# A token-mixing block: z's broadcast behind a q tile, and the low parts of w1 behind `ol`

## The chip, the cores and the metric

The kernel runs on one core of a Trainium2 chip. The metric is the device time of one execution in microseconds. The engines are named as the profile names them: PE (TensorE's matmuls) and PEld (its weight loads), DVE (VectorE), ACT (ScalarE), POOL (GpSimd) and SP (SyncE, which only issues DMAs here).

## The reference

Two blocks follow each other on a sequence of 2048 tokens with 512 channels, in float32. Shown is the core of it; the first block is attention with 32 heads of 16 channels, the second an MLP over the tokens.

```python
h = x + A(layernorm(x)); h2 = h + B(layernorm(h))

# A: linear attention with a learned feature map
q, k, v = split_heads(x @ wqkv)
pq, pk = q @ w_phi, k @ w_phi                      # per head, 16 x 16
phi_q = concat(softmax(pq), softmax(-pq))          # 32 features per head
phi_k = concat(softmax(pk), softmax(-pk))
kv = phi_k^T v;  z = sum over tokens of phi_k
o = (phi_q kv) / (phi_q . z + 1e-6);  out = o @ wo

# B: MLP across the tokens
u = gelu(h^T w1 + b1);  y = u w2 + b2              # w1 2048 x 1792, w2 1792 x 2048
```

## The kernel before, in words

**Numbers in two parts.** Large matmuls run on pairs of float32r tiles: a high part, which ScalarE copies out of the float32 source, and a low part, source minus high part, which VectorE or GpSimd subtracts. `split` (line 54) issues both. `mm3` (line 59) makes one product of three matmuls: high by high, high by low, low by high. So every weight that is streamed from memory costs a ScalarE copy (`whi`, line 56) and a subtraction (`wlo`, line 57).

**Stages.** The 2048 tokens are 16 tiles of 128.
1. Preparation and a loop over k and v tiles (lines 216 to 414): k's projection, its logits (maximum and minimum of each head, two subtractions), exp, sums, normalization on GpSimd (`pk`, line 193) and the sum z over the tiles in `zacc`; v's projection, and kv on TensorE (`kvp`, line 205). Six q tiles are projected in this loop too.
2. A hand-over (lines 416 to 509). The last k and v tiles are finished, wo is split into `woh` (ScalarE, line 426) and `wol` (GpSimd, line 429), and z is broadcast to all partitions: two matmuls of ones with the halves of `zacc` (line 486) and two copies into `zB` (line 487). From here on `ez`, the product of a q tile's features with `zB` on GpSimd (line 440), can be made. q tiles 6, 7, 8 and 9 are projected in this stretch.
3. A software pipeline over the q tiles (the loop `for it in range(NT + 3)`, line 620), described below.
4. The rest of the first MLP matmul (lines 707 to 715), the second one with w2 streamed (from line 756), and the output.

**Who decides the order.** In stage 1 and stage 4 a planner orders each engine's instructions. From line 417 to line 653 the order on PE, DVE, ACT and POOL is that of the program text, `manual_schedule`; each engine takes its instructions strictly in that order. SP's DMAs are ordered by the planner.

**A q tile's way.** `q_mm` projects it into PSUM (tile `pu`, a pool of two buffers, so tile n+2 goes where tile n was). `q_logits` takes the maximum `mx` and the minimum `mn` (lines 151, 152) and subtracts on DVE (line 144); from tile 6 on, the negative half is copied by ACT out of PSUM (line 146) and subtracted later on POOL by `negate` (line 159), to which the list `MN` holds what is due. `q_exp` (line 169, ACT) follows. `q_sums` takes sums on DVE (line 214). `s_den` makes the weights `w` of a tile from `ez` (six DVE instructions, from `tz`, line 449, to `w`, line 455). `s_pq` multiplies the tile by them on POOL (`eq<-eq,w`, line 458).

**One iteration of the loop**, `it`, in order:
- `s_x(it)`: DMA of a tile of x. `s_rstd(it-3)` on POOL: `r` (line 578) and `ve` (line 579).
- `s_num(it-1)`: 32 small matmuls into the PSUM tile `tn` (line 544), and ACT copies its high part, `oh` (line 548).
- `s_wo(it-2)`: 12 matmuls with wo into the one PSUM buffer `po`.
- `s_tr(it)`: 8 transposes into the same `tn` (line 526), two ACT copies `pht` (line 528). They wait until `oh` and `ol` have been read out.
- `lead(it, 1)`: `s_pq(it+1)`, `s_ez(it+3)` and `negate` on POOL, the next `q_mm` on PE, `q_exp` on ACT.
- `run(...)` (line 638): it takes one instruction from each of its lists in turn. The first list is `ol` (DVE subtracts the low part out of `tn`, line 553), then the next tile's logits, then the sums; the second list is `s_den(it+2)`. Then `negate`.
- `s_hn(it-3)`: the normalized tile `hn` and its split `hs`, the low part on POOL (line 57).
- `s_h(it-2)`: DVE adds x to `po` (`h`, line 568, which frees `po`), a DMA stores it, and DVE takes its statistics (`st`, `ve`, lines 571 to 575).
- `fill(p)`: six matmuls of the first MLP product for a pair of hidden blocks; and `fill_load(p)` every second time: `stream` loads two 128x256 blocks of w1, ACT makes `whi`, DVE makes `wlo`, a 128x512 subtraction at line 57. The loads of one iteration's end serve fills that come two iterations later.

In iteration 1 a further q tile is projected between `s_num` and `s_tr` (line 631); it is tile 11.

Of the kernel before, what the change touches and what calls it, by code (L numbers as in the profile page):

```python
# [11 lines left out]
AF = mybir.ActivationFunctionType  # L12
# [7 lines left out]
NT = S // P  # L20
KD = D // P
# [12 lines left out]
def block_kernel(ctx: ExitStack, tc: tile.TileContext, x, xT, wT, phic, wo, w1, b1, w2, b2,  # L34
                 kvmask, ident_in, out):
    nc = tc.nc
# [17 lines left out]
    def split(hi, lo, src, lo_engine):  # L54

        nc.scalar.activation(hi, src, AF.Copy)  # L56
        return lo_engine.tensor_sub(lo, src, hi)  # L57

    def mm3(o, ah, al, bh, bl, first, last):

        nc.tensor.matmul(o, ah, bh, start=first, stop=False)  # L61
        nc.tensor.matmul(o, ah, bl, start=False, stop=False)  # L62
        nc.tensor.matmul(o, al, bh, start=False, stop=last)  # L63
# [24 lines left out]
    zacc = wp.tile([P, NG, P], F32, name="zacc")  # L88
# [5 lines left out]
    X, XH, EQ, PK, VS, SQ, PS, W = {}, {}, {}, {}, {}, {}, {}, {}  # L94

    def load_x(t):
        raw = kk.tile([P, KD, P], F32, name="xraw", bufs=3)
        nc.sync.dma_start(raw, xT[t])
        return raw
# [18 lines left out]
    def proj(t, wh, wl, pool, name, by_part=False):  # L118
        o = pool.tile([P, D], F32, name=name, tag=name)
        if by_part:  # L120
            for i, (a, w) in enumerate(((0, wh), (1, wh), (0, wl))):
                for kt in range(KD):
                    nc.tensor.matmul(o, X[t][:, a, kt, :], w[:, kt, :], start=i == 0 and kt == 0,
                                     stop=i == 2 and kt == KD - 1)
            return o
        for kt in range(KD):
            mm3(o, X[t][:, 0, kt, :], X[t][:, 1, kt, :], wh[:, kt, :], wl[:, kt, :],
                kt == 0, kt == KD - 1)
        return o
# [6 lines left out]
    def logit_ops(src, e, pool):  # L136

        v = src.rearrange("p (j h d) -> p j h d", h=2, d=DH)
        ev = signs(e)
        mx = wk.tile([P, NPR, 2], F32, name="mx")  # L140
        mn = wk.tile([P, NPR, 2], F32, name="mn")

        def shift():
            nc.vector.tensor_sub(ev[:, :, 0], v, mx.unsqueeze(3).to_broadcast([P, NPR, 2, DH]))
            if pool:
                nc.scalar.activation(ev[:, :, 1], v, AF.Copy)  # L146
                MN.append((ev, mn))
            else:
                nc.vector.tensor_sub(ev[:, :, 1], mn.unsqueeze(3).to_broadcast([P, NPR, 2, DH]), v)

        return [lambda: nc.vector.tensor_reduce(mx, v, axis=AX.X, op=ALU.max),
                lambda: nc.vector.tensor_reduce(mn, v, axis=AX.X, op=ALU.min),
                shift]

    def negate():

        if MN:
            ev, mn = MN.pop(0)
            nc.gpsimd.tensor_sub(ev[:, :, 1], mn.unsqueeze(3).to_broadcast([P, NPR, 2, DH]), ev[:, :, 1])

    def run(*lists):

        for i in range(max(map(len, lists))):
            for ops in lists:
                if i < len(ops):
                    ops[i]()
# [42 lines left out]
    def q_sum(t):  # L209

        assert t < SUMS or t - SUMS in W, "a tile's sums would go where others are still wanted"
        SQ[t] = sums[:, t % SUMS]
        e = signs(EQ[t])
        return [lambda c=c: nc.vector.reduce_sum(SQ[t][:, :, 1 - c], e[:, :, c], axis=AX.X) for c in range(2)]
# [144 lines left out]
    def q_mm():  # L359
        if q["mm"] < NT:  # L360
            PS[q["mm"]] = proj(q["mm"], wqh, wql, ps_q, "pu")
            q["mm"] += 1

    def q_logits(lag):
        n = q["logits"]
        if n < min(NT, q["mm"] - lag + NT * (q["mm"] == NT)):
            EQ[n] = big.tile([P, NG, P], F32, name="eq", tag="big")
            q["logits"] += 1
            return logit_ops(PS[n], EQ[n], n >= len(Q_AT))
        return []  # L370
# [7 lines left out]
    def q_sums(lag):  # L378
        n = q["sum"]
        if n < min(NT, q["exp"] - lag + NT * (q["exp"] == NT)):  # L380
            q["sum"] += 1
            return q_sum(n)
        return []

    def v_kv():

        nonlocal v
        v_proj(v)
        if v % 2 == 0:
            kv(v - 2)  # L390
            kv(v - 1)
        v += 1
# [4 lines left out]
    for t in range(3, NT - 1):  # L397
        if t + 2 < NT:
            raw = load_x(t + 2)
# [25 lines left out]
    def wo_hi(j):  # L425
        nc.scalar.activation(woh[:, j], WO[j], AF.Copy)

    def wo_lo(j):
        nc.gpsimd.tensor_sub(wol[:, j], WO[j], woh[:, j])
# [8 lines left out]
    def s_ez(t):  # L438
        EZ[t] = az.tile([P, NG, P], F32, name="ez")
        nc.gpsimd.tensor_mul(EZ[t], EQ[t], zB)  # L440
# [33 lines left out]
    k_norm(NT - 1, False)  # L474
    for j in range(KD):
        wo_hi(j)
    wo_lo(0)
    wo_lo(1)
    v_kv()
    run(q_logits(0))  # L480
    nc.vector.tensor_add(zacc, zacc, PK[NT - 1])
    negate()
    zB = big.tile([P, NG, P], F32, name="zB", tag="big")
    for g in range(2):
        pz = ps_k.tile([P, 4, P], F32, name="pk_ps")
# [2 lines left out]
    q_exp(0)  # L488
    s_ez(0)
    s_ez(1)  # L490
    wo_lo(2)
    wo_lo(3)
    q_mm()
    v_kv()
    run(s_den(0))
    run(q_logits(0))
# [40 lines left out]
    def s_num(t):  # L537

        pn = ps_t.tile([P, 2, 4, P], F32, name="tn")[:, :, 0:2]
        for b in range(2):  # L540
            for c in range(4):
                for r in range(2):
                    rows, cols = slice(64 * r, 64 * r + 64), slice(32 * c, 32 * c + 32)
                    nc.tensor.matmul(pn[cols, r, b, :], kvB[rows, b, cols], PHT[t][rows, 4 * b + c, :],  # L544
                                     start=True, stop=True, skip_group_check=True)
        oh = ak.tile([P, 2, 2, P], F32R, name="oh")
        ol = ak.tile([P, 2, 2, P], F32R, name="ol")
        nc.scalar.activation(oh, pn, AF.Copy)
        OS[t] = oh, ol, pn

    def s_ol(t):
        oh, ol, pn = OS[t]
        return [lambda: nc.vector.tensor_sub(ol, pn, oh)]
# [7 lines left out]
    def s_x(t):  # L561
        HT[t] = ak.tile([P, D], F32, name="h", bufs=4)
        nc.sync.dma_start(HT[t], x[t * P:(t + 1) * P, :])
# [13 lines left out]
    def s_rstd(t):  # L577
        nc.gpsimd.tensor_tensor(r2[:, t:t + 1], VE[t][:, 0:1], mhalf[:, :1], op=ALU.pow)
        nc.gpsimd.tensor_mul(VE[t][:, 1:2], VE[t][:, 1:2], r2[:, t:t + 1])
# [7 lines left out]
    w1v = w1.rearrange("(k p) f -> p k f", p=P)  # L587
    w2v = w2.rearrange("(k p) s -> p k s", p=P)

    def stream(src, k0, n, c0, w):  # L590

        raw = wf.tile([P, n, w], F32, name="wraw")
        wh_ = wf.tile([P, n, w], F32R, name="whi")
        wl_ = wf.tile([P, n, w], F32R, name="wlo")
        nc.sync.dma_start(raw, src[:, k0:k0 + n, c0:c0 + w])
        LO.append(split(wh_, wl_, raw, nc.vector).ins)
        return wh_, wl_

    PU, WI, LO = {}, {}, []
    FN, FL = [0] * (NF // 2), [0] * (NF // 2)  # L600

    def fill_load(p):
        if FL[p] < NT:
            WI[p, FL[p]] = stream(w1v, FL[p], 2, p * 256, 256)
            FL[p] += 2

    def fill(p, pool=None):

        t = FN[p]
        FN[p] = t + 1  # L610
        if FL[p] <= t:
            fill_load(p)
        if t == 0:
            PU[p] = [pool.tile([P, D], F32, name="pu", tag="pu") for _ in range(2)]
        a, b = WI[p, t - t % 2]
        for c in range(2):
            mm3(PU[p][c], a[:, t % 2, c * P:(c + 1) * P], b[:, t % 2, c * P:(c + 1) * P],
                HN[t][:, 0], HN[t][:, 1], t == 0, t == NT - 1)

    for it in range(NT + 3):  # L620
        if 0 <= it < NT:
            s_x(it)
        if 0 <= it - 3 < NT:
            s_rstd(it - 3)
        if 0 <= it - 1 < NT:
            s_num(it - 1)
        if 0 <= it - 2 < NT:
            s_wo(it - 2)
        if it == 1:
            run(q_logits(0))  # L630
            q_mm()
        if 0 <= it < NT:
            s_tr(it)
        if it == 0:
            s_kv()
        lead(it, 1)
        den = s_den(it + 2) if it + 2 < NT else []
        run((s_ol(it - 1) if 0 <= it - 1 < NT else []) + q_logits(1) + (q_sums(0) if it > 0 else []), den)
        if it > 0:
            negate()  # L640
        if 0 <= it - 3 < NT:
            s_hn(it - 3)
        if 0 <= it - 2 < NT:
            s_h(it - 2)
        if FN[0] <= it - LAG:
            fill(0, ps_f)
        for _ in range(2):
            if q["logits"] == NT and FN[1] <= it - LAG:
                fill(1, ps_q)
        for p in range(2):  # L650
            if it >= LAG - 2 and FL[p] <= FN[p] + 1:
                fill_load(p)
    ms.close()
    a2.close()
    aq.close()
# [195 lines left out]
```

## Time and profile before

| What | Value |
|---|---|
| median of 3 runs | 536.01 us (535.8 to 536.05) |
| the profiled execution's own time | 535.76 us |
| its span in the trace | 534.0 us |
| granted TensorE clock, mean | 0.997 |
| busy: PE, PEld | 522.6 us, 450.4 us |
| busy: DVE, ACT, POOL | 393.5, 258.6, 236.6 us |
| moved from and to memory | 55.84 MB, 103 GB/s over the span |

How to read it: times are microseconds from the start of the span; a busy matmul row is not TensorE at its peak, as the matmuls are pipelined and their ends are modelled. The stages lie at about 0 to 115 (stage 1), 115 to 144 (stage 2), 144 to 275 (stage 3) and 275 to 534 (stage 4). A row of the timeline gives start, duration, engine, line, operation, the tile written and the tiles read, shapes, a count, and in brackets how long the engine had been idle and what ended that. An instruction that waits after it was taken up shows the wait as part of its duration.

### The profile page before, as it was taken

Reading aid. Unit: us, or ns where it says so; the run is one execution under the profiler, and the core shown is the slowest. Engines: PE = TensorE matmul, PEld = TensorE weight load, DVE = VectorE, ACT = ScalarE, POOL = GpSimd, SP = SyncE. Lnnn points to the kernel's source line nnn. Section 1 sums busy time; section 2 is a strip of 40 time slices with the busy share of each in tenths; the row PEclk is TensorE's granted clock in tenths of the full one; section 3 lists DMA queues with packets and bytes.
Section 4 is the critical chain, followed back from the end, with each engine's and each line's share of the span. In section 5 each row is a group of like instructions: output and inputs, shape, how many; then the busy total and the mean of one; then the engine's idle time right before and its main releaser. Section 6 shows DMA issues by size and latency. Waiting matters only on the chain.

```text
span 534.0 us, 9892 instructions
## 1 busy us (share of the span) xinstructions
PE 522.6 (98%) x3872; PEld 450.4 (84%) x3872; DVE 393.5 (74%) x722; ACT 258.6 (48%) x406; POOL 236.6 (44%) x184
## 2 busy tenths in 40 slices
PE   8999999998999999999999999999999999999995
PEld 7888888886876777778788888888899999999995
DVE  6993999875699989986536523835768878888774
ACT  6998844434346555544546423525443343343340
POOL 2589699878978989985435000000001101100110
PEclk9999999999999999999999999999999999999998
DMA  8534300021302233333256333533014556536631
GB/s 315 196 113 118 99 21 21 1 78 63 97 4 86 73 101 118 100 121 118 91 166 179 98 100 97 160 107 91 20 41 108 139 149 144 133 119 140 138 80 40
DMA packets 45486, 55.84 MB, mean 105 GB/s; under 512 B 3968, under 2 KB 33024, under 8 KB 45440
## 3 DMA queue, kind: packets, MB, share of 16 engines
q1 hardware_dynamic: 43136, 51.38, 30.2%
q0 software_dynamic: 2016, 3.67, 5.1%
q8 instruction: 30, 0.49, 0.4%
q10 hardware_dynamic: 288, 0.17, 0.1%
q14 instruction: 16, 0.13, 0.1%
HBM read 46.81 MB, written 8.39 MB: 103 GB/s over the span
## 4 chain that ended last, share of the span: by engine, by line
PE 91%; DVE 5%; ACT 2%; issue 1%; POOL 0%; DVEq 0%; POOLq 0%
PE py L745 26%; PE pu L61 12%; PE pu L62 12%; PE pu L63 12%; PE po L61 3%; PE pv L62 3%; PE pv L63 3%; PE pv L61 3%; PE pk_ps L61 2%; PE pk_ps L63 2%; PE pk_ps L62 2%; PE tn L526 2%; PE po L62 2%; PE po L63 2%; PE kvp L205 2%; PE tn L544 1%
## 5 line engine op out<-in xcount | busy, mean ns | idle before, releaser
L57 DVE TENSOR_TENSOR wlo<-wraw,whi 128x512 fp32r<-128x512 f32 (+1 forms) x84 | 100.3, 1204 | 69.4 <-ACT whi L56 67.9
L56 ACT ACTIVATE whi<-wraw 128x512 fp32r<-128x512 f32 (+1 forms) x84 | 81.9, 987 | 127.1 <-PE py L745 73.8
L783 POOL DMA_DIRECT2D out<-ot x14 | 12.5, 1001 | 211.3 <-DVE ot L781 211.3
L745 PE MATMUL py<-uf,whi 128*128 128x256 f32 x560 | 96.2, 283 | 0.0
L61 PE MATMUL pu<-hs,whi 128*128 128x512 f32 x224 | 87.6, 394 | 0.6 <-ACT eq L146 0.6
L62 PE MATMUL pu<-hs,whi 128*128 128x512 f32 x224 | 87.2, 389 | 0.0
L63 PE MATMUL pu<-hs,wlo 128*128 128x512 f32 x224 | 86.8, 389 | 0.0
L745 PEld LDWEIGHTS py<-uf,whi 128*128 128x128 f32 x560 | 83.3, 192 | 0.0
L745 PE MATMUL py<-uf,wlo 128*128 128x256 f32 x280 | 69.9, 283 | 0.0
L61 PEld LDWEIGHTS pu<-hs,whi 128*128 128x128 f32 x224 | 42.1, 188 | 9.5 <-ACT eq L146 1.1
L745 PEld LDWEIGHTS py<-uf,wlo 128*128 128x128 f32 x280 | 49.7, 192 | 0.0
L63 PEld LDWEIGHTS pu<-hs,wlo 128*128 128x128 f32 x224 | 42.0, 188 | 8.8
L62 PEld LDWEIGHTS pu<-hs,whi 128*128 128x128 f32 x224 | 42.1, 188 | 8.2
L528 ACT ACTIVATE pht<-tn 128x512 f32<-128x512 f32 x32 | 17.4, 596 | 49.7 <-PE tn L526 49.7
L440 POOL TENSOR_TENSOR ez<-eq,zB 128x1024 f32<-128x1024 f32 x16 | 38.4, 2406 | 0.7 <-ACT zB L487 0.7
L745 PE MATMUL py<-un,whi 128*128 128x256 f32 x224 | 38.4, 283 | 0.0
L193 POOL TENSOR_TENSOR pk<-pk,sk 128x1024 f32<-128x1024 f32 x16 | 31.1, 1944 | 9.4 <-DVE sk L192 7.6
L745 PEld LDWEIGHTS py<-un,whi 128*128 128x128 f32 x224 | 33.2, 192 | 0.1
L458 POOL TENSOR_TENSOR eq<-eq,w 128x1024 f32<-128x1024 f32 x16 | 31.1, 1942 | 3.1 <-DVE w L455 3.1
L197 POOL TENSOR_TENSOR zacc<-zacc,pk 128x1024 f32<-128x1024 f32 x13 | 31.3, 2409 | 0.6
L57 POOL TENSOR_TENSOR hs<-hn,hs 128x512 fp32r<-128x512 f32 x16 | 20.6, 1291 | 21.1 <-ACT hs L56 21.1
L61 PE MATMUL po<-woh,oh 128*128 128x512 f32 x64 | 26.6, 416 | 1.0 <-DVE h L568 1.0
(161 smaller groups left out, 1144.3 us busy)
## 6 DMA issues: line engine op xcount, KB each, us to landing
wraw<-in_w SPq DMA_DIRECT2D x112, 256.0 KB, 2.8
xraw<-in_xT SPq DMA_DIRECT2D x16, 256.0 KB, 3.1
xh<-in_x SPq DMA_DIRECT2D x16, 256.0 KB, 2.7
h<-in_x SPq DMA_DIRECT2D x16, 256.0 KB, 2.9
out<-h SPq DMA_DIRECT2D x16, 256.0 KB, 2.2
out<-ot POOLq DMA_DIRECT2D x14, 256.0 KB, 4.8
wraw<-in_wT SPq DMA_DIRECT2D x12, 256.0 KB, 4.9
wo<-in_wo SPq DMA_DIRECT2D x4, 256.0 KB, 3.8
```

The source lines that it names most:

```text
L56: nc.scalar.activation(hi, src, AF.Copy)
L57: return lo_engine.tensor_sub(lo, src, hi)
L61: nc.tensor.matmul(o, ah, bh, start=first, stop=False)
L62: nc.tensor.matmul(o, ah, bl, start=False, stop=False)
L63: nc.tensor.matmul(o, al, bh, start=False, stop=last)
L193: nc.gpsimd.tensor_mul(heads(PK[t]), heads(PK[t]), sk.unsqueeze(2).to_broadcast([P, 2 * H, DH]))
L197: nc.gpsimd.tensor_add(zacc, zacc, PK[t])
L440: nc.gpsimd.tensor_mul(EZ[t], EQ[t], zB)
L458: nc.gpsimd.tensor_mul(heads(EQ[t]), heads(EQ[t]), W[t].rearrange("p g c h -> p (g c h)").unsqueeze(2).to_broadcast([P, 2 * H, DH]))
L528: nc.scalar.activation(PHT[t][:, half * 4:half * 4 + 4, :], ptr[:, half], AF.Copy)
L745: nc.tensor.matmul(o, a[x], b[:, y], start=start and i == 0, stop=stop and i == 2, skip_group_check=True)
L783: nc.gpsimd.dma_start(out[(t + i) * P:(t + i + 1) * P, :], flat(ot[:, i]), accum_op=ALU.add)
```

## The change

- `run` takes the maximum over a generator instead of `map`, so that it can be called with one list.
- Stage 2: the four low parts of wo come later on POOL. `wo_lo(0)` stands behind `negate`, the other three behind `s_ez(1)`; before, two stood ahead of the v tile and two behind `s_ez(1)`. The last addition into `zacc` is made in two halves on DVE. The projection of q tile 7 (`q_mm`) stands ahead of z's two matmuls instead of behind `s_ez(1)`.
- `stream` issues the DMA and the ACT copy, and puts the subtraction on the list `LATER`. `flush` issues what is on the list, in order, on DVE. It is called right behind `ol` in each iteration, at a load that a fill needs at once, and once behind the loop. `ol` is issued alone; the logits and the sums then take turns with `s_den` in a second `run`.

```diff
@@ run
-        for i in range(max(map(len, lists))):
+        for i in range(max(len(x) for x in lists)):
@@ stage 2
     for j in range(KD):
         wo_hi(j)
-    wo_lo(0)
-    wo_lo(1)
     v_kv()
     run(q_logits(0))
-    nc.vector.tensor_add(zacc, zacc, PK[NT - 1])
+    for g in range(2):
+        nc.vector.tensor_add(zacc[:, 4 * g:4 * g + 4, :], zacc[:, 4 * g:4 * g + 4, :], PK[NT - 1][:, 4 * g:4 * g + 4, :])
     negate()
+    wo_lo(0)
+    q_mm()
     zB = big.tile([P, NG, P], F32, name="zB", tag="big")
...
     q_exp(0)
     s_ez(0)
     s_ez(1)
-    wo_lo(2)
-    wo_lo(3)
-    q_mm()
+    for j in range(1, KD):
+        wo_lo(j)
     v_kv()
@@ the loads of w1
+    LATER = []
+
+    def flush():
+        while LATER:
+            wl_, raw, wh_ = LATER.pop(0)
+            LO.append(nc.vector.tensor_sub(wl_, raw, wh_).ins)
...
         nc.sync.dma_start(raw, src[:, k0:k0 + n, c0:c0 + w])
-        LO.append(split(wh_, wl_, raw, nc.vector).ins)
+        nc.scalar.activation(wh_, raw, AF.Copy)
+        LATER.append((wl_, raw, wh_))
         return wh_, wl_
...
         if FL[p] <= t:
             fill_load(p)
+            flush()
@@ the loop
         den = s_den(it + 2) if it + 2 < NT else []
-        run((s_ol(it - 1) if 0 <= it - 1 < NT else []) + q_logits(1) + (q_sums(0) if it > 0 else []), den)
+        run(s_ol(it - 1) if 0 <= it - 1 < NT else [])
+        flush()
+        run(q_logits(1) + (q_sums(0) if it > 0 else []), den)
...
             if it >= LAG - 2 and FL[p] <= FN[p] + 1:
                 fill_load(p)
+    flush()
```

## The prediction

> **What bounds the kernel now.** I read the first part of the page, then TensorE's waits, then the loop of line 620 cut into windows (columns: stretch; its length; busy time of PE, PEld, DVE, ACT, POOL; granted clock; DMA share; GB/s).
>
> ```profile
> PE 522.6 (98%) x3872; PEld 450.4 (84%) x3872; DVE 393.5 (74%) x722; ACT 258.6 (48%) x406; POOL 236.6 (44%) x184
> ```
> ```profile
> PE pk_ps L486 <- DVE zacc L481: 1.7, 1, 1.7
> ...
> PE tn L526 <- DVE ol L553: 0.5, 1, 0.5
> ```
> ```profile
> 165.00:205.00 40.00, 37.74 (x327) 29.04 (x326) 37.76 (x81) 23.04 (x37) 34.34 (x27) 1.00 0.29 93
> 205.00:235.00 30.00, 30.00 (x263) 23.75 (x263) 28.69 (x66) 14.51 (x25) 27.90 (x24) 1.00 0.40 124
> ```
>
> TensorE is busy 98% of the span; the change aims at two of its waits, 1.7 us at z's broadcast (L486) and 0.5 us at the transposes of L526. But the last two rows say what an average hides: from 165 to 235 VectorE is busy 37.8 of 40 and 28.7 of 30 us, GpSimd 34.3 and 27.9. In this stretch three engines are full, and whatever VectorE loses can reach TensorE.
>
> **Part 1: the order around z's broadcast.** GpSimd first, then VectorE, TensorE (with one row of the chain that ended last) and ScalarE.
>
> ```profile
> 123.96 3.48 POOL L429 TENSOR_TENSOR wol<-wo,woh 128x512 fp32r<-128x512 f32 x2
> ...
> 129.13 4.77 POOL L440 TENSOR_TENSOR ez<-eq,zB 128x1024 f32<-128x1024 f32 x2 [0.68 <-ACT zB L487]
> 133.85 2.54 POOL L429 TENSOR_TENSOR wol<-wo,woh 128x512 fp32r<-128x512 f32 x2
> ...
> 145.85 1.08 POOL L159 TENSOR_TENSOR eq<-mn,eq 128x512 f32<-128x512 f32 x1
> ```
> ```profile
> 124.03 2.28 DVE L481 TENSOR_TENSOR zacc<-zacc,pk 128x1024 f32<-128x1024 f32 x1
> ```
> ```profile
> 126.46 1.96 PE L486 MATMUL pk_ps<-zacc,ones 128*128 128x512 f32 x4 [1.69 <-DVE zacc L481]
> ...
> 148.86 0.50 PE L61 MATMUL pu<-wqh,xs 128*128 128x512 f32 x1
> ```
> ```profile
> 128.65 0.23 PE pu L62
> ```
> ```profile
> 125.74 0.59 ACT L146 ACTIVATE eq<-pu 128x512 f32<-128x512 f32 x1
> 128.45 0.60 ACT L487 ACTIVATE zB<-pk_ps 128x512 f32<-128x512 f32 x1 [0.26 <-PE pk_ps L486]
> 146.96 1.16 ACT L169 ACTIVATE eq<-eq,r 128x1024 f32<-128x1024 f32 x1 [0.23 <-POOL eq L159]
> 148.02 0.57 ACT L146 ACTIVATE eq<-pu 128x512 f32<-128x512 f32 x1
> ```
>
> TensorE: q tile 7 starts where the wait of 1.69 began, at some 124.7, and its 12 matmuls at 0.23 bring z to about 127.4 instead of 126.46. The wait on zacc is gone: the two halves begin at 124.03 as the whole did, and with no GpSimd instruction beside them are done before 126.3, when it was.
>
> GpSimd: tile 6's negation (L159) needs ScalarE's copy, which ends at 126.33. Before, two low parts of wo filled the time to 127.4 (123.96 + 3.48); now GpSimd stands idle to 126.4, negates, does one low part (2.54 / 2 = 1.25) and waits for zB. zB's second half comes 1.99 us after z's start, lasts 0.60 and is there at 130.0 instead of 129.05: +0.98 for ez. Three low parts are left behind ez instead of two: +1.25. From ez to tile 8's negation (145.85 to 146.93) the trace shows no idle time on GpSimd, so that negation ends **2.2 us later**, at 149.16.
>
> Who waits: ScalarE's exp of tile 8 stands right behind that negation (146.96, waiting for POOL), and behind exp, in order, the copy of q9 out of PSUM (148.02 to 148.59). q11 goes into the PSUM buffer that this copy frees (two buffers), and began at 148.86, 0.27 behind it. With exp at 149.19 the copy ends at 150.82 and q11 starts at about 150.95. So the time saved at z is lost again by then, whatever TensorE did in between, and the sum has **+2.1**. Even if GpSimd were not late at all, q11 could not gain more than the 0.27. VectorE's first reduction of q11 and all behind it wait too, as the new interleaving puts that reduction ahead of tz: VectorE is 2.1 late as well at ol of tile 1.
>
> The edit of the max in the helper costs nothing, and the order of SyncE's DMAs I take as hidden: the trace shows no wait of TensorE for one, and the loads come at least an iteration ahead of their matmuls.
>
> **Part 2: w1's low parts behind ol.** Number and kind stay (128x512 on VectorE). What changes is what they meet on GpSimd. Iteration 9, VectorE, ScalarE, GpSimd, TensorE; then GpSimd's path with nothing beside it:
>
> ```profile
> 212.01 1.76 DVE L57 TENSOR_TENSOR wlo<-wraw,whi 128x512 fp32r<-128x512 f32 x2
> 213.70 0.68 DVE L553 TENSOR_TENSOR ol<-tn,oh 128x512 fp32r<-128x512 f32 x1
> 214.30 1.21 DVE L449 TENSOR_REDUCE tz<-ez 128x64 f32<-128x1024 f32 x1
> ...
> 218.14 0.68 DVE L568 TENSOR_TENSOR h<-po,h 128x512 f32<-128x512 f32 x1
> ```
> ```profile
> 212.08 0.60 ACT L548 ACTIVATE oh<-tn 128x512 fp32r<-128x512 f32 x1
> ```
> ```profile
> 211.32 1.31 POOL L57 TENSOR_TENSOR hs<-hn,hs 128x512 fp32r<-128x512 f32 x1
> 212.56 1.02 POOL L578 TENSOR_TENSOR r<-ve,mhalf 128x1 f32<-128x1 f32 x1
> 213.80 1.94 POOL L458 TENSOR_TENSOR eq<-eq,w 128x1024 f32<-128x1024 f32 x1
> ```
> ```profile
> 219.06 0.50 PE L61 MATMUL po<-woh,oh 128*128 128x512 f32 x1
> ```
> ```profile
> 220.03 0.55 POOL L578 TENSOR_TENSOR r<-ve,mhalf 128x1 f32<-128x1 f32 x1 [0.39 <-DVE ve L575]
> ...
> 220.80 1.94 POOL L458 TENSOR_TENSOR eq<-eq,w 128x1024 f32<-128x1024 f32 x1
> ```
>
> What two such instructions do to each other stands later in the trace:
>
> ```profile
> 291.56 1.23 DVE L57 TENSOR_TENSOR un<-u,un 128x1024 fp32r<-128x1024 f32 x1 [0.58 <-ACT un L56]
> 292.70 1.23 DVE L57 TENSOR_TENSOR wlo<-wraw,whi 128x512 fp32r<-128x512 f32 x1
> ```
> ```profile
> 291.66 1.72 POOL L692 TENSOR_TENSOR tt<-u,tt 128x256 f32<-128x256 f32 x1
> ```
>
> GpSimd's 128x256 subtraction, issued 0.1 us behind VectorE's, lasts to 293.38: it sits until VectorE's ends (about 292.75). VectorE's next low part, issued at 292.70, lasts to 293.93: it sits until GpSimd's has ended. So they **take turns**, a whole instruction each, and one that already waits goes ahead of the other engine's next. zacc shows it as well: 2.28 us at 124.03, 0.07 behind a wol on GpSimd.
>
> Before, the low parts stood where GpSimd had only the end of hs and the tiny r and ve: two cost 1.70 (212.01 to 213.70). Behind ol they meet eq<-eq,w (1.94) and ez (2.4, half of the 4.77 at 129.13). In iteration 9 ol could begin at oh's end, 212.68, the first low part 0.60 later (213.70 to 214.30 is that step) at 213.28; eq<-eq,w comes at 212.56 + 0.77 (220.03 to 220.80) = 213.33.
> - VectorE first: low part to 213.95, eq to 215.87, second low part to 216.5, tz at 216.45 instead of 214.30. h is 2.2 late and ends at 221.0; TensorE wants its po buffer at 219.06. Stall **2.0**.
> - GpSimd first: eq to 215.25, low part 215.9, ez 218.3, low part 218.9. Stall **4.4**.
>
> The same working for the other iterations with two low parts (3, 7, 11), from these rows:
>
> ```profile
> 164.24 1.28 DVE L57 TENSOR_TENSOR wlo<-wraw,whi 128x512 fp32r<-128x512 f32 x2
> ...
> 170.97 0.68 DVE L568 TENSOR_TENSOR h<-po,h 128x512 f32<-128x512 f32 x1
> ```
> ```profile
> 171.71 0.50 PE L61 MATMUL po<-woh,oh 128*128 128x512 f32 x1 [1.03 <-DVE h L568]
> ```
> ```profile
> 197.18 1.30 POOL L57 TENSOR_TENSOR hs<-hn,hs 128x512 fp32r<-128x512 f32 x1 [2.20 <-ACT hs L56]
> ...
> 225.51 1.29 POOL L57 TENSOR_TENSOR hs<-hn,hs 128x512 fp32r<-128x512 f32 x1 [0.41 <-ACT hs L56]
> ```
> ```profile
> 198.05 0.58 ACT L548 ACTIVATE oh<-tn 128x512 fp32r<-128x512 f32 x1
> ...
> 226.39 0.60 ACT L548 ACTIVATE oh<-tn 128x512 fp32r<-128x512 f32 x1
> ```
>
> - Iteration 3: oh is there early, the first low part is 0.60 behind the end of st's chain and eq<-eq,w at least 0.77, so VectorE leads by 0.17, and its second low part waits one eq<-eq,w: 1.94. h already holds TensorE up here (1.03): all of it goes through, **+2.0**.
> - Iteration 7: eq at 197.18 + 1.24 (hs to r, 211.32 to 212.56) + 0.77 = 199.19, low part at 198.05 + 0.58 + 0.60 = 199.23: GpSimd leads by 0.04. **+1.85** if VectorE is first after all, 2.4 more if not (one ez). The 0.5 us at L526 goes, and TensorE then waits at po instead.
> - Iteration 11: 227.52 against 226.39 + 1.20 = 227.59, GpSimd leads by 0.07: **+2.0**, or 2.4 more.
> - Iterations 5 and 6 have one low part, worth **+0.4** (one eq<-eq,w in 6, mostly inside po's slack); 13 has no ez, **+0.5**; later ones nothing, GpSimd being half empty.
>
> The sum: 2.1 + 2.0 + 0.4 + 1.85 + 2.0 + 2.0 + 0.5 = 10.9 with VectorE first each time, 18.1 with GpSimd first in 7, 9 and 11. The leads (0.04, 0.05 the other way, 0.07) are too small to call; by their signs two of three are lost. I take the middle, **+14.4**. The profiled execution took 535.76 (span 534.0, 1.8 around it; median of the runs 536.01): 535.76 + 14.4 = **550.2**.
>
> A rule that makes it worse: stalls of 3.0 us (iteration 3: 1.03 + 2.0) to 4.7 (iteration 7, GpSimd first: 4.25 + 0.5) would be TensorE's longest. In this trace the granted clock is 1.00 wherever matmuls run, and falls behind the last one:
>
> ```profile
> 528.00:531.00 3.00, 0.50 (x5) 0.29 (x3) 2.10 (x6) 0.00 (x0) 0.00 (x0) 0.97 0.19 72
> 531.00:534.00 3.00, 0.00 (x0) 0.00 (x0) 0.00 (x0) 0.00 (x0) 0.00 (x0) 0.50 0.30 105
> ```
>
> Full to about 530.8 and 0.50 behind it gives the 0.97: some 2.3 us after the last matmul. How long the clock stays down once work is back, no row shows; if as long as such a stall, 3.2 us at half speed is 1.6 lost each, 2 to 3 times. The Trainium skill (TensorE: Matmul & The Clock Gate, Part 1) has the clock halved after an idle window of about 3.4 us and full again after about as long of work; the drop at the end agrees in kind, and by that rule the cost would be 1.7 each, as an estimate from the page.
>
> **The rivals.**
> - *Back to back*: VectorE's second low part does not let GpSimd in between. For it: the two at 212.01 ran with only 0.5 lost; against it: 292.70. Then 3 and 9 cost nothing, 7 and 11 one eq<-eq,w each if GpSimd leads: 2.1 + 0.4 + 1.8 + 1.9 = 6.2, **542.0**; 538.3 if VectorE leads always.
> - *The clock falls in the long stalls*: 14.4 + 3 x 1.6, **555.0**. For it: the drop at the end. Against: the stalls may stay at 2 to 3 us.
> - *Faster*: ScalarE's copy of q9 is not what q11 waits for, so the gain at z lives. Its place is iteration 1, its price between the 0.27 of q11's lead and the 1.69 at z, say 0.7, and 0.5 at L526, with the low parts slipping past eq<-eq,w unharmed; it decides if tile 8's negation ends no later than the 146.93 of now: 535.76 - 1.2 = **534.6**. Against: GpSimd's unbroken queue from 129.13.
> - *Nothing*: late engines swallow gain and loss, **535.8**.
>
> **How the numbers follow.** Taking turns, 546.7 to 553.9: 0.55. Back to back: 0.20. Clock as well: 0.12. Faster: 0.08. Nothing: 0.05. The range runs from 538.0, which takes in the back-to-back case whole, to 556.0, and leaves out the last two and half of what lies above. Below 0.2% (1.1 us) a measurement can't tell a change: faster 0.08, same 0.05, slower 0.87.
>
> **What would show it.** Right: no wait at L486, but one of some 2.4 us (2.1, and the 0.3 that TensorE is early) at q11 (L61) on L146; wlo of L57 at 128x512 well over its 0.68 between 165 and 260, eq<-eq,w or ez beside it; TensorE waiting for h (L568) in iterations 3, 7, 9, 11. Wrong: tile 8's negation at 147; low parts of 0.7 us behind ol; no wait for L568. Then VectorE's time from 165 to 235 was not the bound that I take it for.

## The result, and the profile after

The changed kernel takes **556.34 us** (median of 6 runs, 555.26 to 559.76), the kernel before 535.99 (6 runs, 535.8 to 536.45): a ratio of 1.0386, 95% interval 1.0356 to 1.0416. It is slower by 20.3 us. The forecast was 550.2, from 538.0 to 556.0, so the direction was right and the time lies 0.34 above the top of the range. The profiled execution took 555.36 (span 553.6, granted clock 0.990 where it was 0.997).

First the page of the changed kernel, TensorE's row and the clock in forty slices:

```profile
PE 528.2 (95%) x3872; PEld 454.8 (82%) x3872; DVE 402.7 (73%) x723; ACT 258.0 (47%) x406; POOL 234.8 (42%) x184
PEclk9999999999999998898999999999999999999999
```

TensorE has as many instructions as before and 5.6 us more of busy time, and VectorE's one instruction more, 9.2 us: part of VectorE's "work" is now waiting. Three slices show a granted clock below 0.9. TensorE's waits, those that are new or grew (engine, line, what it waited for, total, times, longest):

```profile
PE po L61 <- DVE h L568: 14.1, 6, 4.6
PE pu L61 <- ACT eq L146: 2.8, 2, 2.1
PE kvp L205 <- ACT vs L184: 1.3, 1, 1.3
```

The waits at z and at L526, 2.2 us together, are gone, as the change wants. In their place stand 14.1 us at `po` for VectorE's `h` (1.0 before), a wait of 2.1 at q11 and 1.3 at kv.

Where the time went is read from the starts of the same TensorE instructions in both kernels. Those of before that the prediction did not need, with the first fill behind the first of them (208.40, used below):

```profile
204.75 0.50 PE L61 MATMUL po<-woh,oh 128*128 128x512 f32 x1
...
208.40 0.48 PE L61 MATMUL pu<-hs,whi 128*128 128x512 f32 x1
...
233.36 0.50 PE L61 MATMUL po<-woh,oh 128*128 128x512 f32 x1
...
247.67 0.50 PE L61 MATMUL po<-woh,oh 128*128 128x512 f32 x1
```

The changed kernel, q11 first and then the first matmul with wo behind each h, with the first fill (`pu`) behind the three long waits:

```profile
151.42 0.50 PE L61 MATMUL pu<-wqh,xs 128*128 128x512 f32 x1 [2.14 <-ACT eq L146]
...
174.84 0.50 PE L61 MATMUL po<-woh,oh 128*128 128x512 f32 x1 [1.47 <-DVE h L568]
...
212.00 0.79 PE L61 MATMUL po<-woh,oh 128*128 128x512 f32 x1 [4.57 <-DVE h L568]
212.59 0.63 PE L62 MATMUL po<-wol,oh 128*128 128x512 f32 x1
213.01 0.63 PE L63 MATMUL po<-woh,ol 128*128 128x512 f32 x1
...
217.11 0.48 PE L61 MATMUL pu<-hs,whi 128*128 128x512 f32 x1
...
231.58 0.50 PE L61 MATMUL po<-woh,oh 128*128 128x512 f32 x1 [3.70 <-DVE h L568]
...
236.81 0.48 PE L61 MATMUL pu<-hs,whi 128*128 128x512 f32 x1
...
251.28 0.50 PE L61 MATMUL po<-woh,oh 128*128 128x512 f32 x1 [3.70 <-DVE h L568]
...
256.54 0.49 PE L61 MATMUL pu<-hs,whi 128*128 128x512 f32 x1
...
267.62 0.50 PE L61 MATMUL po<-woh,oh 128*128 128x512 f32 x1 [0.32 <-DVE h L568]
```

| TensorE instruction | before | after | late by | of this, new in the step |
|---|---|---|---|---|
| q11 | 148.86 | 151.42 | 2.56 | 2.56 |
| wo behind the h of iteration 3 | 171.71 | 174.84 | 3.13 | 0.57 |
| wo behind the h of iteration 7 | 204.75 | 212.00 | 7.25 | 4.12 |
| of iteration 9 | 219.06 | 231.58 | 12.52 | 5.27 |
| of iteration 11 | 233.36 | 251.28 | 17.92 | 5.40 |
| of iteration 13 | 247.67 | 267.62 | 19.95 | 2.03 |

The span is 19.6 longer, so nothing is lost behind the loop. Of q11's 2.56 the change does not explain all: this execution was 0.76 late already when GpSimd normalized the last k tile, ahead of anything that part 1 moves. The first row is of before, the second of after:

```profile
122.06 1.94 POOL L193 TENSOR_TENSOR pk<-pk,sk 128x1024 f32<-128x1024 f32 x1 [1.08 <-PE pu L63]
```
```profile
122.82 1.94 POOL L193 TENSOR_TENSOR pk<-pk,sk 128x1024 f32<-128x1024 f32 x1 [1.09 <-PE pu L63]
...
130.69 4.76 POOL L440 TENSOR_TENSOR ez<-eq,zB 128x1024 f32<-128x1024 f32 x2 [1.25 <-ACT zB L488]
135.41 3.79 POOL L429 TENSOR_TENSOR wol<-wo,woh 128x512 fp32r<-128x512 f32 x3
...
148.65 1.05 POOL L159 TENSOR_TENSOR eq<-mn,eq 128x512 f32<-128x512 f32 x1
```

The rest is part 1, step by step as it was worked out: GpSimd waits for zB, three low parts stand behind ez, and tile 8's negation comes at 148.65 instead of 145.85. ScalarE then shows exp waiting for it, and the copy that frees q11's buffer behind exp:

```profile
149.73 1.15 ACT L169 ACTIVATE eq<-eq,r 128x1024 f32<-128x1024 f32 x1 [2.64 <-POOL eq L159]
150.79 0.58 ACT L146 ACTIVATE eq<-pu 128x512 f32<-128x512 f32 x1
```

Part 2 shows in VectorE's and GpSimd's rows: iteration 3, then 7, 9 and 11.

```profile
167.78 1.28 DVE L595 TENSOR_TENSOR wlo<-wraw,whi 128x512 fp32r<-128x512 f32 x2
...
202.41 5.23 DVE L595 TENSOR_TENSOR wlo<-wraw,whi 128x512 fp32r<-128x512 f32 x2
...
211.26 0.68 DVE L568 TENSOR_TENSOR h<-po,h 128x512 f32<-128x512 f32 x1
...
222.07 5.15 DVE L595 TENSOR_TENSOR wlo<-wraw,whi 128x512 fp32r<-128x512 f32 x2
...
241.77 5.14 DVE L595 TENSOR_TENSOR wlo<-wraw,whi 128x512 fp32r<-128x512 f32 x2
```
```profile
167.91 0.60 POOL L579 TENSOR_TENSOR ve<-ve,r 128x1 f32<-128x1 f32 x1
168.47 2.39 POOL L458 TENSOR_TENSOR eq<-eq,w 128x1024 f32<-128x1024 f32 x1
...
202.35 1.94 POOL L458 TENSOR_TENSOR eq<-eq,w 128x1024 f32<-128x1024 f32 x1
204.24 2.85 POOL L440 TENSOR_TENSOR ez<-eq,zB 128x1024 f32<-128x1024 f32 x1
...
221.93 1.94 POOL L458 TENSOR_TENSOR eq<-eq,w 128x1024 f32<-128x1024 f32 x1
...
241.63 1.94 POOL L458 TENSOR_TENSOR eq<-eq,w 128x1024 f32<-128x1024 f32 x1
```

Read iteration 7 as taking turns. eq<-eq,w begins at 202.35, 0.06 ahead of the low parts, and lasts to 204.29; the first low part sits until then and ends at some 204.9 (worked out, as the two low parts stand in one row). ez, taken up at 204.24, has its 2.4 us only behind that, to 207.09 (2.85). The second low part sits through all of ez and ends at 207.64. Two subtractions of 0.68 took 5.23 us, and everything behind them on VectorE, `h` at its end, is late. In iterations 9 and 11 GpSimd leads by 0.14 each, with the same outcome.

Behind the three stalls something is lost that is no wait (windows: stretch; length; busy PE, PEld, DVE, ACT, POOL; granted clock; DMA share; GB/s):

```profile
205.00:212.00 7.00, 2.43 (x42) 1.57 (x40) 6.79 (x11) 3.10 (x5) 3.35 (x2) 0.98 0.37 115
212.00:216.00 4.00, 4.00 (x11) 3.18 (x12) 3.93 (x8) 0.00 (x0) 2.77 (x4) 0.60 0.17 66
231.50:236.00 4.50, 4.42 (x12) 3.45 (x13) 4.33 (x11) 0.00 (x0) 3.18 (x4) 0.62 0.16 60
251.30:256.00 4.70, 4.70 (x15) 3.71 (x16) 4.38 (x12) 0.00 (x0) 3.48 (x4) 0.65 0.14 56
```

The clock is down in the matmuls behind each stall. Some seven of the 12 with wo start 0.42 to 0.43 apart (212.59, 213.01) instead of 0.23. From the first matmul with wo to the first fill it takes 5.11, 5.23 and 5.26 us (212.00 to 217.11, 231.58 to 236.81, 251.28 to 256.54), where it took 3.65 before (204.75 to 208.40): 1.5, 1.6 and 1.6 lost, together **4.7 us** which no instruction of the change contains.

### The profile page after: what moved, and what is told of

Same layout as the page of the kernel before. It is cut to its first block, busy times and chain, and to the rows that moved or that the text cites. A ratio compares the mean times of both kernels' runs of the same rounds, so it can differ in the third digit from the quotient of the medians.

```text
span 553.6 us, 9886 instructions
## 1 busy us (share of the span) xinstructions
PE 528.2 (95%) x3872; PEld 454.8 (82%) x3872; DVE 402.7 (73%) x723; ACT 258.0 (47%) x406; POOL 234.8 (42%) x184
## 4 chain that ended last, share of the span: by engine, by line
PE 79%; DVE 12%; ACT 4%; POOL 3%; issue 1%; DVEq 0%; POOLq 0%
PE py L757 25%; PE pu L61 10%; PE pu L63 9%; PE pu L62 9%; DVE wlo L595 3%; PE pk_ps L61 2%; PE pv L62 2%; PE po L61 2%; PE pk_ps L62 2%; PE pk_ps L63 2%; PE pv L63 2%; PE pv L61 2%; PE po L63 2%; PE po L62 2%; POOL ez L440 2%; DVE tz L449 1%
## 5 line engine op out<-in xcount | busy, mean ns | idle before, releaser
L595 DVE TENSOR_TENSOR wlo<-wraw,whi 128x512 fp32r<-128x512 f32 x56 | 53.8, 972 | 46.1 <-ACT whi L603 41.9
L56 ACT ACTIVATE whi<-wraw 128x1792 fp32r<-128x1792 f32 x28 | 47.7, 1704 | 77.9 <-PE py L757 73.8
L57 DVE TENSOR_TENSOR wlo<-wraw,whi 128x1792 fp32r<-128x1792 f32 x28 | 56.6, 2022 | 16.8 <-ACT whi L56 16.6
L603 ACT ACTIVATE whi<-wraw 128x512 fp32r<-128x512 f32 x56 | 34.4, 627 | 49.4 <-PE pu L62 45.3
L61 PE MATMUL po<-woh,oh 128*128 128x512 f32 x64 | 28.6, 447 | 14.2 <-DVE h L568 14.1
L440 POOL TENSOR_TENSOR ez<-eq,zB 128x1024 f32<-128x1024 f32 x16 | 40.1, 2507 | 1.2 <-ACT zB L488 1.2
```

What stands on the lines that cost most here:

```text
L595: LO.append(nc.vector.tensor_sub(wl_, raw, wh_).ins)
L603: nc.scalar.activation(wh_, raw, AF.Copy)
```

## The experiments

**The theories.** Mine: the time is (a) about 2 us of part 1, through GpSimd's late negation; (b) some 12 us of part 2, VectorE and GpSimd taking turns over the two low parts behind `ol`; (c) some 4 to 5 us of the lower clock behind the stalls. The rival to (a) is that the q tile in front of z helps and the rest hides; to (b) that the low parts are late for what comes behind them (their own order, h, the loads) whatever GpSimd does; to (c) that a slower matmul behind a stall is hidden by the next wait, as VectorE decides anyway.

### Part 1 alone

The stage-2 hunk of the diff put into the kernel before; loads and loop as before.

> Only the first part of the change: q tile 7 ahead of z, zacc in halves, wo's low parts behind it on GpSimd; w1's low parts stay where they were. Theory: GpSimd's queue from zB to tile 8's negation is 2.2 us late, exp and the copy of q9 behind it, so q11 on TensorE starts 1.8 to 2.1 us later than before, and the whole is 2 us slower, 538. Rival: the gain of 1.7 at z lives when the loop is left alone: 534.3.

Measured: 539.18 (539.07 to 539.32), against 536.3 of before beside it: ratio 1.0052, 1.0037 to 1.0067. Part 1 alone loses 2.9 us. q11 in its profile, and the clock behind it:

```profile
150.62 0.50 PE L61 MATMUL pu<-wqh,xs 128*128 128x512 f32 x1 [2.15 <-ACT eq L146]
```
```profile
150.60:154.00 3.40, 3.38 (x9) 2.71 (x10) 1.82 (x2) 0.94 (x2) 3.40 (x3) 0.60 0.00 0
```

q11 is 1.76 late (150.62 against 148.86), without the 0.76 of the other execution. The rival, a gain, is refuted. What I had not counted: here the clock already fell behind q11's wait of 2.15, which costs eight matmuls their 0.2 us, 1.6. The Trainium skill (TensorE: Matmul & The Clock Gate, Part 1) has the clock halved after an idle window of about 3.4 us. This wait is shorter, with 1.3 us of waiting at kv some 5 us before it, and the clock fell all the same; here the measurement decides. Five of the profiled kernels have this wait of 2.13 to 2.16 at q11: four show the slow matmuls behind it, the full change does not. What decides between the two is not shown.

### Part 2 alone

The changed kernel with its stage-2 hunk undone.

> Only the second part: w1's low parts behind ol, stage 2 as before. Theory of turns at a shared port: the loop loses by itself what it lost in the changed kernel, in iterations 6, 7, 9, 11 and 13, with the three long stalls and the clock's drop behind them: 536 + 17 to 18 = 553 to 554. Rival: the loop only loses because stage 2 left the engines out of step; alone it costs at most 2: 538.

Measured: 554.14 (552.64 to 555.59), ratio 1.0322, 1.0299 to 1.0345. TensorE's waits:

```profile
PE po L61 <- DVE h L568: 14.1, 6, 4.6
PE pk_ps L486 <- DVE zacc L481: 1.7, 1, 1.7
```

The same 14.1 at `po`, and z's wait is back. 17.8 alone and part 1's 2.9 alone make 20.7, the whole change costs 20.3: the parts add up, neither hides the other. Behind the three long stalls of this profile (mean clock 0.984) 2.2, 1.6 and 2.6 us are lost, read as above: the size of a clock drop varies.

### Low parts that do not meet GpSimd

The subtraction in the loop takes its second operand from PSUM; the low parts of w1 hold other numbers than the reference needs (`raw` minus what the tile of sums holds, which q's sums overwrite as the loop goes).

```diff
+    nc.vector.memset(sums, 0.0)
...
+    IN_LOOP = [1]
@@ flush
-            LO.append(nc.vector.tensor_sub(wl_, raw, wh_).ins)
+            src = sums.rearrange("p (k s) g c h -> p k (s g c h)", k=2) if IN_LOOP else wh_
+            LO.append(nc.vector.tensor_sub(wl_, raw, src).ins)
...
+    IN_LOOP.clear()
```

> The changed kernel, but the subtraction of w1's low parts inside the loop reads its second operand from PSUM (the tile of sums, filled with zeros at the start) instead of the high part in SBUF, so the low parts hold other numbers; number, shape and place of the instructions stay. Theory of the port: with one operand in SBUF VectorE and GpSimd no longer take turns, each low part takes its 0.68 us and the stalls at h go: 538 to 539, what the first part costs. Rival (the place: low parts ahead of tz and h make h late whatever they read): over 548.

Measured: 539.26 (538.62 to 539.98), ratio 1.0054, 1.0039 to 1.0069. Place, order, number and shape of the low parts are those of the change; 17 of the 20 us are gone. Iteration 7 in VectorE's rows, what GpSimd ran beside it, and TensorE's wait at `po`:

```profile
203.24 1.27 DVE L598 TENSOR_TENSOR wlo<-wraw,smq 128x512 fp32r<-128x512 f32 x2
```
```profile
203.17 1.94 POOL L459 TENSOR_TENSOR eq<-eq,w 128x1024 f32<-128x1024 f32 x1
```
```profile
PE po L61 <- DVE h L569: 2.8, 3, 1.5
```

1.27 instead of 5.23, 2.8 instead of 14.1. GpSimd leads here too, by 0.07, and neither engine waits for the other. So the late place itself costs nothing; what costs is the second SBUF operand beside a running GpSimd instruction. That agrees with the Trainium skill (SBUF — State Buffer, "Who interferes with whom"): VectorE with two SBUF inputs and GpSimd reading SBUF exclude each other for a whole instruction, whoever issues first blocks the other, and with at most one SBUF input, outside its 2-port modes, VectorE does not contend.

### GpSimd two tiny instructions later

```diff
-    cst.tile([P, 56], F32, name="pad")
+    tiny = cst.tile([P, 56], F32, name="pad")
@@ s_rstd, behind ve
+        for i in range(2):
+            nc.gpsimd.tensor_mul(tiny[:, i:i + 1], mhalf[:, 0:1], mhalf[:, 1:2])
```

> The changed kernel with two tiny instructions (128x1) on GpSimd between ve and eq<-eq,w in each iteration, which put eq<-eq,w about 0.3 us later; nothing is left out. Theory of turns: GpSimd led by 0.06 to 0.14 us in iterations 7, 9 and 11, now VectorE's first low part leads, two low parts cost 3 us instead of 5.2, the stalls fall to about 2 us, the clock stays at 1.00: 545 to 547. Rival (lateness of GpSimd alone counts): 556 or a little more.

Measured: 539.87 (538.82 to 540.02), ratio 1.0061, 1.0046 to 1.0076. Two useless 128x1 instructions take 16.5 us off. I had expected some 10 of it: VectorE first, one eq<-eq,w between the two low parts. VectorE and GpSimd in iteration 7:

```profile
203.56 1.32 DVE L597 TENSOR_TENSOR wlo<-wraw,whi 128x512 fp32r<-128x512 f32 x2
```
```profile
203.54 0.79 POOL L581 TENSOR_TENSOR pad<-mhalf 128x1 f32<-128x1 f32 x2
204.29 2.39 POOL L458 TENSOR_TENSOR eq<-eq,w 128x1024 f32<-128x1024 f32 x1
```

The two tiny ones take 0.34 where nothing is beside them and 0.79 here: one of them sat behind the first low part and had its turn then. The turn that eq<-eq,w would have taken was used up, the second low part came next, and eq<-eq,w waited for that (2.39 instead of 1.94). This also explains iteration 3 of the changed kernel, where `ve` does it by chance: 0.60 long instead of 0.19, low parts 1.28, eq<-eq,w 2.39.

### TensorE kept busy in the stalls

Fourteen matmuls of zeros, added into the bank of the fills, ahead of wo in iterations 8, 10 and 12; they leave the result as it is.

```diff
-    wqp.tile([P, 504], F32, name="pad")
+    zero = wqp.tile([P, 504], F32, name="pad")
+    nc.vector.memset(zero, 0.0)
@@ s_wo
+        if t in (6, 8, 10):
+            for _ in range(14):
+                nc.tensor.matmul(PU[0][0], zero[:, 0:P].bitcast(F32R), HN[0][:, 0], start=False, stop=False,
+                                 skip_group_check=True)
```

> The changed kernel with 14 more matmuls by a tile of zeros (they add nothing to the first MLP sum) ahead of wo's in the iterations 8, 10 and 12, whose stalls were 4.6, 3.7 and 3.7 us; 14 x 0.23 = 3.2 us of each stall is then work. Theory: each long stall halves TensorE's clock for some 3 us behind it, 1.4 us lost three times; without idle time the clock stays at 1.00 and the time falls by about 4: 552. Rival: the clock's drop hides behind VectorE, which sets the pace there: 556.

Measured: 550.87 (550.56 to 552.24), ratio 1.0282, 1.0268 to 1.0296, against 536.07 beside it. VectorE's two low parts in iteration 7, and the same two stretches as above:

```profile
203.51 5.23 DVE L600 TENSOR_TENSOR wlo<-wraw,whi 128x512 fp32r<-128x512 f32 x2
```
```profile
205.00:212.00 7.00, 6.89 (x60) 5.02 (x58) 6.86 (x9) 3.97 (x6) 4.49 (x3) 1.00 0.38 115
212.00:216.00 4.00, 2.90 (x13) 2.35 (x14) 3.86 (x10) 0.00 (x0) 1.67 (x3) 1.00 0.17 66
```

More work on TensorE, and 5.5 us less at the median: the two low parts still took 5.23, but the clock stays at 1.00 behind them. Three of its four executions had a mean clock of 1.000 and took 550.56 to 550.97, some 4.6 less than the three of the changed kernel at 0.990; that is the 4.7 read from the matmuls. The fourth is the profiled one (552.24, clock 0.995), whose clock fell behind q11's wait as in part 1 alone. The rival, that the next wait hides slow matmuls, is refuted. The executions of the changed kernel spread with the clock too: 0.990 gave 555.3 to 555.4, 0.984 and 0.981 gave 557.24, 0.978 gave 559.76.

### All low parts of wo on VectorE

Three versions made from the kernel before. Loads and loop are as they were there, zacc is added in halves as in the change, and the low parts of wo leave GpSimd for VectorE. In the first, q tile 7 is ahead of z as in the change; in the second behind, as before; the third is the second with the first load of one pair of hidden blocks an iteration later.

```diff
@@ wo_lo
-        nc.gpsimd.tensor_sub(
+        nc.vector.tensor_sub(
@@ stage 2: behind negate(), no wo_lo elsewhere
+    for j in range(KD):
+        wo_lo(j)
@@ third version alone
-            if it >= LAG - 2 and FL[p] <= FN[p] + 1:
+            if it >= LAG - 2 + p and FL[p] <= FN[p] + 1:
```

> Before, with q tile 7 ahead of z, zacc in halves and all four low parts of wo on VectorE, which stood idle there, instead of GpSimd; w1's low parts as before. Theory: the loss of the first part came from GpSimd's lateness (1.0 us by the later zB, 1.25 by the low part moved behind it); here GpSimd has no low part left behind ez, tile 8's negation comes 1 us earlier than before, q11 does not wait, and the gain at z lives: 534.6, 1.4 faster than before. Rival (q tile 7 ahead of z is what costs): 538 to 539, as with the first part alone.

> As the one before, but z's matmuls stay ahead of q tile 7. With no GpSimd instruction beside it the halved addition is done 1 us earlier, z starts 0.3 to 0.8 us behind the v tile instead of 1.7, and ez some 1.5 us earlier than before. Theory: 1 to 1.4 faster than before, 534.7, and no worse than with q tile 7 first. Rival: TensorE only waits elsewhere, 536.

> As the one before, and the second pair's first load of w1 comes an iteration later (3 instead of 2), so that VectorE has one low part instead of two in iteration 3, where h holds TensorE up by 1.03 us. Theory (VectorE sets the pace there): 0.6 us less, 534.1. Rival (the wait moves to iteration 4): the same as the one before.

Measured, against 536.07: q tile first 534.99 (ratio 0.9982, 0.9973 to 0.9991), z first 534.66 (0.9973, 0.9962 to 0.9983), z first with the later load **533.62** (0.9958, 0.9945 to 0.997). All three lie below both kernels, the first by 0.18%, at the edge of what can be told. Tile 8's negation, and in the first q11 too; then the second:

```profile
145.32 1.06 POOL L159 TENSOR_TENSOR eq<-mn,eq 128x512 f32<-128x512 f32 x1
```
```profile
148.10 0.50 PE L61 MATMUL pu<-wqh,xs 128*128 128x512 f32 x1 [0.86 <-ACT eq L146]
```
```profile
144.15 1.07 POOL L159 TENSOR_TENSOR eq<-mn,eq 128x512 f32<-128x512 f32 x1
```

With GpSimd relieved the negation comes 0.5 and 1.7 ahead of the 145.85 of before, and the gain lives: q11 starts at 148.10 and 147.83 instead of 148.86. In the first version it still waits 0.86, which was not expected, and in the second not at all. The q tile in front of z, which ends TensorE's wait there, delays zB and with it ez, and takes 1.2 of that back. That its place costs time at the end is not shown: the two intervals overlap. The third version took TensorE's wait at `po` in iteration 3 from 1.0 to 0.7 in the profile; its executions (533.6 to 534.13) all lie below those of the second (534.22 to 534.95), but the two intervals overlap, and 0.3 at `po` does not account for the 1.0 between the medians.

## Why the prediction missed, step by step

- **What bounds the kernel** held. Where three engines were full, what VectorE lost reached TensorE: 14.1 of waits for h.
- **Part 1, +2.1.** Right, and by the steps named: 1.8 in the changed kernel (2.56 less the 0.76 that this execution brought along) and 1.76 alone; in three more profiles with this stage 2 the same subtraction gives 1.4 to 1.8. The wait of 2.1 stands at the place that was named. The limit of 0.27 for a gain at q11 held only for a negation that stays where it was; the last three versions moved it forward.
- **Iteration 3, +2.0.** Wrong in size: 0.57 in the table, and the low parts took 1.28. That VectorE leads was right; that eq<-eq,w takes the next turn was not. `ve`, 0.13 behind the first low part, took it. The working put eq<-eq,w into the race and left out the tiny instruction ahead of it, which takes a turn like a large one.
- **Iterations 7, 9 and 11, +5.85 or +13.05.** The mechanism was right, taking turns as at 291.56. By the signs of the leads two of three were lost; I took the middle, and GpSimd was first by 0.06, 0.14 and 0.14 in all three. The stalls are 4.57, 3.70 and 3.70, sum 11.97, against 4.75 (4.25 and the 0.5 of L526), 4.4 and 4.4 worked out for that outcome. The term was undersized: the middle of 5.85 and 13.05 is 9.45, and 11.5 came (11.97 less the 0.5 saved at L526).
- **The clock behind the stalls** is the step that failed most. It was named, priced at 1.6 and put among the rivals with a chance of 0.12, as "the stalls may stay at 2 to 3 us", and so it was in no term of the sum. It came three times, at 1.5 to 1.6 each: 4.7. The price was right and the place in the sum was not: it was no rival to taking turns but its consequence, once GpSimd is first. The wait at q11 was given no such price either; in part 1 alone it cost 1.6.
- **Iterations 5, 6 and 13, +0.9.** Iterations 5 and 6 show no wait at `po` for the 0.4 foreseen; iteration 13's wait is 0.32 for 0.5.
- **The rivals.** "Back to back" is refuted by 5.23 us for two low parts. "Faster" failed by its own condition, the negation at 148.65 and not at 146.93. "Nothing" failed with both parts measured alone.

Added up as measured, TensorE's 19.95 at iteration 13 are 0.76 that this execution brought along, 1.8 of part 1, 0.57 in iteration 3, 12.3 of waits in iterations 7, 9, 11 and 13 less the 0.5 saved at L526, 4.7 of the clock, and some 0.3 in pieces too small to place. Of the forecast's terms part 1 was 0.3, iteration 3 1.4 and iterations 5, 6 and 13 together 0.6 too high, and the races 2.0 too low. By luck these nearly cancel; what remains of the miss is the clock's 4.7 and the 0.76. One more wait was not in it: 1.3 at kv for ScalarE's `vs`, which stands behind the exp of tile 7 and so behind GpSimd's queue in the same way. It comes ahead of q11's wait and costs nothing of its own, as q11's buffer is what decides there.

## What to carry to other kernels

Before an instruction of VectorE with two SBUF operands is moved, look at what GpSimd runs at the new place, the tiny instructions too, and count whole instructions of it as waits; one operand in PSUM, or another engine's turn spent on something tiny, takes that cost away. When two instructions race within 0.1 us in several iterations, price each outcome and don't count on the races going half and half. When the working gives TensorE a stall of some 2 to 5 us, put the slow matmuls behind it in the sum and not among the rivals.

## What the runs showed of the hardware beyond that

- A 128x1 instruction on GpSimd uses up a turn like a large one: 5.23 us for two low parts without it, 1.32 with it.
- Behind stalls of 3.70 and 4.57 us some seven matmuls of 512 columns ran at 0.43 instead of 0.23 apart. They begin at once or up to some 1.5 us later (251.28 to 252.81), and one such drop cost 1.5 to 2.6 us (the changed kernel and part 2 alone). Behind waits of 2.13 to 2.16 us they came in four of five profiles; behind one of 1.21 us, left over when TensorE was kept busy, they did not come.
- Profiled executions differ by up to 0.9 us at 122 us, ahead of both parts of the change: the last k tile's normalization began at 122.06 in the kernel before, 122.82 in the changed one, and in the eight experiments anywhere from 122.02 (part 1 alone) to 122.93 (part 2 alone). Between the first two it arises at once: the 16 matmuls that begin at 5.3 us take 2.82 in the changed kernel and 2.02 in the one before. What sets it is not shown.
